# Sink keys inside the own-key tiles of batches 2 and 3, and a written TensorE order, in a sliding-window attention and FFN kernel

## The chip, the core and the metric

The kernel runs on one core of one Trainium2 chip. A core has five engines with one in-order instruction stream each: TensorE (PE: matmuls and their weight loads), VectorE (DVE), ScalarE (ACT), GpSimd (POOL) and SyncE (SP). POOL, SP and ACT also issue DMA transfers, which sixteen DMA engines carry out. The metric is the device time of one execution in microseconds (us), the median of several runs.

## The reference

There are four batches of eight heads, 768 queries each, with a head size of 64. A query sees the keys of its window (itself and the 127 before it) and the first four keys of the sequence, the sinks. The attention output of all heads, as 3072 tokens by 512, goes through a gated feed-forward net.

```python
scores = scale * np.matmul(q, k.transpose(0, 1, 3, 2))
is_sink = pos[None, :] < int(n_sink)              # n_sink = 4
in_window = (rel >= 0) & (rel < int(window))      # rel = query - key, window = 128
scores = np.where(is_sink | in_window, scores, -1000000000.0)
a = np.exp(scores - np.max(scores, axis=-1, keepdims=True))
a = a / (np.sum(a, axis=-1, keepdims=True) + 1e-09)
attn = np.matmul(a, v)                            # 4 x 8 x 768 x 64
# x = attn as (3072, 512)
h = (x @ w1) * (x @ w2) @ w3                      # w1, w2: 512 x 1024, w3: 1024 x 1024
out = h @ w_out                                   # w_out: 1024 x 512
```

## The kernel before

Everything is cast to bf16 and multiplied on TensorE. `w3 @ w_out` is folded into one 1024 x 512 matrix first: `fold_w3` (task `t3`, four transposes of 128 x 128 each) and `fold_mm` (task `fm`, two matmuls of 512 columns each). Then each batch goes through attention, the two gate products (task `g`, four matmuls for 128 hidden units and one chunk of tokens) and the projection (task `p`, eight matmuls of 512 columns for 128 tokens).

Attention works on scores with keys in the partitions. Queries and keys arrive as tokens by head dimensions and are turned by TensorE (`transposes`, task `tpk`, eight transposes for 128 tokens; batches 0 and 1) or by DMA (`transposes_dma`, tasks `tdk` and `tdq`, issued on SP; batches 2 and 3, list `XPOSE`). Two heads share the 128 rows of the array, 64 rows each, so score matmuls come in pairs that run side by side. For a tile `t` of 256 queries and a pair of heads `r`, `scores` (task `sc`, L254) multiplies the key blocks before, at and after the tile's middle: six matmuls for a `t` above 0, four for `t` = 0. ACT takes the exponential, DVE multiplies with a 0/1 mask, and `values` (task `av`, L334) multiplies the result with the values. A value row carries a 1 behind its 64 numbers, so column 65 of the product is the sum by which DVE divides (`rec`, L354 and L357). Batch 0 has a variant of the two in blocks of 128 queries (L273, L298).

The sinks go another way in tiles with `t` above 0. `sink_scores` (task `ss`, L237) multiplies the four sink keys of all eight heads, laid out in `ksbd`, in four matmuls of 32 columns of weights; ACT takes the exponential into `es`, and `values` adds one matmul of 130 columns per 128 queries, from `es` and the sink values `vs`. `sink_keys` and `sink_values` prepare `ksbd` and `vs` on DVE.

The attention output is turned again, by TensorE (task `xt`, batch 0) or by DMA (`x_transposes_dma`, task `xd`, L374, on SP), since the gate products take it with the dimensions in the partitions.

POOL casts while it loads: `load_qkv` (L108) issues one DMA each for 128 tokens of k, q and v. The weights to be folded come over SP as fp32 (`load_raw`) and are cast by DVE and ACT. Before the first of them has come, `keep_busy` (L464) multiplies the zeros of `idle`, which is `ksbd[3]`, set first of all by DVE (L173 and L174).

The order of all engines but POOL comes from a planner in the kernel (`plan`, L674). Each task has stages with an engine and an estimated duration, the tasks that it comes after, and the loads that it needs, with landing times from `landings` (L484). The planner walks through time; ACT, DVE and SP take what is ready first, and `pe_pick` (L689) chooses for TensorE the task with the least wait and the best priority, with a margin for `av` and a pace for `sc`. The planner's times set only the order; on the chip each engine goes through its list and waits by semaphores. Score tiles share two PSUM buffers (`ps_sc`), everything else four (`ps_mm`, ring `mm`).

Of the kernel before, what the change touches and what calls it, by code (L numbers as in the profile page):

```python
# [21 lines left out]
def kernel(  # L22
# [13 lines left out]
    nc = tc.nc  # L36
# [19 lines left out]
    SINKS = (1, 3)  # L56
# [15 lines left out]
    vc = const.tile([P, B, D], FP32, name="vc")  # L72
    maskt = const.tile([P, 2, 512], BF16, name="maskt")
# [5 lines left out]
    wo_sb = wp.tile([P, KFF, DM], BF16, name="wo_sb")  # L79
# [9 lines left out]
    vN = per_batch("vN", [P, NB, H, VS], 3)  # L89
# [5 lines left out]
    ksbd = per_batch("ksbd", [P, 648], 4)  # L95
    vs = per_batch("vs", [P, H, D + 1], 4)
    es = per_batch("es", [P, 512], 2)


    def rows(src, b, kb):  # L100
        return src[b, :, kb * P:(kb + 1) * P, :].rearrange("h p d -> p h d")
# [5 lines left out]

    def load_qkv(b, kb):  # L108
        for src, dst in zip(kqv, (heads(kN[b][:, kb, :]), heads(qN[b][:, kb, :]), vN[b][:, kb, :, 0:D])):
            nc.gpsimd.dma_start(out=dst, in_=rows(src, b, kb))  # L110
# [18 lines left out]
    def load(what, *i):  # L129
        if what == "qkv":  # L130
            if i[1] == 0:
                nc.gpsimd.memset(vN[i[0]][:, :, :, D:D + 1], 1.0)
            for kb in range(i[1], i[2]):
                load_qkv(i[0], kb)
        elif what == "w3":
            load_rows(w3_sb, what, *i)
        elif what == "wo":
            load_rows(wo_sb, what, *i)
        else:
            for dst, src in ((w1_sb, moe_w1), (w2_sb, moe_w2)):  # L140
                load_w(dst, src, i[0] * 256, i[1] * 256)
# [7 lines left out]
    order = [("w3", 6, 8), ("qkv", 0, 0, 1), ("qkv", 0, 1, 2), ("w3", 5, 6), ("qkv", 0, 2, 3),  # L149
             ("qkv", 0, 3, 4), ("w12", 0, 1), ("w12", 1, 2), ("w12", 2, 3), ("w12", 3, 4), ("qkv", 0, 4, 5),  # L150
             ("qkv", 0, 5, 6), ("qkv", 1, 0, 6), ("qkv", 2, 0, 6), ("qkv", 3, 0, 6)]

    nudge = {("g", 0, 1, 5, 0): -300, ("g", 1, 0, 6, 1): 60, ("p", 3, 5, 256): -300, ("g", 2, 0, 3, 0): -300}
# [19 lines left out]
    idle = ksbd[B - 1]  # L173
    nc.vector.memset(idle[:], 0.0)  # L174
# [3 lines left out]
    for b in range(B - 1):  # L178
        nc.vector.memset(ksbd[b][:], 0.0)
# [4 lines left out]
    m4 = maskt[:].rearrange("p v (a c q) -> p (v a) c q", c=2, q=P)  # L184
    nc.gpsimd.affine_select(m4[:, :, 0, :], m4[:, :, 0, :], compare_op=ALU.is_ge, fill=0.0,
                            base=-1, pattern=[[0, 4], [-1, P]], channel_multiplier=1)
    nc.gpsimd.affine_select(m4[:, :, 1, :], m4[:, :, 1, :], compare_op=ALU.is_ge, fill=0.0,
                            base=0, pattern=[[0, 4], [1, P]], channel_multiplier=-1)
    nc.gpsimd.memset(maskt[0:4, 0, P:3 * P], 1.0)
# [7 lines left out]
    for b in range(B):  # L197
        nc.gpsimd.tensor_copy(vs[b][:, :, D], ones_s[:])
    for h in range(H):
        r0 = 32 * (h // 2) + 4 * (h % 2)  # L200
        nc.sync.dma_start(out=vc[r0:r0 + 4, :, :], in_=v[:, h, 0:4, :].rearrange("b s d -> s b d"))
    if hold:
        nc.gpsimd.tensor_copy(spent[:], casts[hold - 1][1][:, 0:1])
    for x in order:
        if x[0] != "qkv" or x[1] == 0:
            load(*x)

# [10 lines left out]
    def transposes_dma(src, dst, kb):  # L218

        nc.sync.dma_start_transpose(out=dst[:, :, kb * P:(kb + 1) * P], in_=src[:, kb, :])  # L220
        yield
# [31 lines left out]

    def scores(b, r, t):  # L254
# [13 lines left out]
        mk = maskt[:, min(t, 1):min(t, 1) + 1, c0:].to_broadcast([P, 2, 512 - c0])  # L268
# [4 lines left out]
    def block_scores(b, j, r0, r1):  # L273
# [3 lines left out]
        for r in range(r0, r1):  # L277
            for s, kb in enumerate(kbs):
                for e in range(2):
# [8 lines left out]
        n, v, c = len(kbs) * P, min(j // 2, 1), (P, 2 * P)[j] if j < 2 else 0  # L288
        nc.vector.tensor_mul(am[:].rearrange("p e (r x) -> p (e r) x", x=n),
                             ex[:].rearrange("p e (r x) -> p (e r) x", x=n),  # L290
                             maskt[:, v:v + 1, c:c + n].to_broadcast([P, 2 * (r1 - r0), n]))
# [6 lines left out]
    def block_values(b, j, r0):  # L298
# [17 lines left out]
        rec = work.tile([P, 2, 2, 1], FP32, tag="rec", name="rec")  # L316
        nc.vector.reciprocal(rec[:], av[:, :, :, D:D + 1])
        if i == 0 and r0 == 0:
            xns[b, t] = work.tile([P, 2, NP, 2, D], BF16, tag="xn", bufs=3, name="xn")
        nc.vector.tensor_mul(xns[b, t][:, i, r0:r0 + 2, :, :], av[:, :, :, 0:D],  # L320
                             rec[:].to_broadcast([P, 2, 2, D]))
# [12 lines left out]
    def values(b, r, t):  # L334
# [18 lines left out]
        rec = work.tile([P, 2, 2, 1], FP32, tag="rec", name="rec")  # L353
        nc.vector.reciprocal(rec[:], av[:, :, :, D:D + 1])  # L354
        if r == 0:
            xns[b, t] = work.tile([P, 2, NP, 2, D], BF16, tag="xn", bufs=3, name="xn")
        nc.vector.tensor_mul(xns[b, t][:, :, r, :, :], av[:, :, :, 0:D],  # L357
                             rec[:].to_broadcast([P, 2, 2, D]))
# [15 lines left out]
    def x_transposes_dma(b, t, i):  # L374

        q0 = t * 256 + i * P
        nc.sync.dma_start_transpose(out=xT[b][:, :, q0:q0 + P],
                                    in_=xns[b, t][:, i].rearrange("p r e d -> p (r e d)"))
# [24 lines left out]
    def fold_w3(i, j0, j1):  # L403
# [5 lines left out]
        if i not in w3T:  # L409
            w3T[i] = (flat((kN, qN)[i - 4][1], "k s")[:, 2048:3072].rearrange("p (k n) -> p k n", n=P)  # L410
                      if i in (4, 5) else work.tile([P, KFF, P], BF16, tag="w3t", bufs=4, name="w3t"))
# [52 lines left out]
    def keep_busy(n):  # L464

        pz = ps_mm.tile([P, 512], FP32, tag="mm", name="pz")
        for _ in range(n):
            nc.tensor.matmul(pz[:], idle[:, 0:P], idle[:, 0:512], start=True, stop=True)
# [5 lines left out]
    def service(what, *i):  # L474
        if what == "qkv":
            return [(0.95 if i[0] == 0 else 0.87, 0.845 if 6 * i[0] + kb < 14 else 2.1, [(x, i[0], kb)])
                    for kb in range(i[1], i[2]) for x in "kqv"]
# [6 lines left out]
    def landings(RAW=2.0, POOL=3.0, DGE=1.3, RAMP=(0.75, 1.0)):  # L484
# [6 lines left out]
        while any(at[n] < len(q) for n, q in queues.items()):  # L491
# [11 lines left out]
            for n in busy:  # L503
# [3 lines left out]
                if left[n][at[n]] <= 0.0:  # L507
                    lag, keys = queues[n][at[n]][2:]
                    for key in keys:
                        arrive[key] = now + lag + min(2.5, max(0.0, 0.25 * (now - 36.0))) + min(3.0, max(0.0, 0.1 * (now - 70.0)))  # L510
# [51 lines left out]
    last_av = []  # L562
    for b in range(B):
        for t in range(NT):
# [3 lines left out]
            for kb in kbs:  # L568
# [5 lines left out]
                else:  # L574
                    qk.append(("tpk", b, kb))
                    task(qk[-1], 1, transposes(b, kb), [("pe", 0.45), ("dve", 0.65)],
                         war, [("k", b, kb), ("q", b, kb)], "mm")
            if t == 0:
# [35 lines left out]
            for r in range(NP):  # L614
                after = list(qk)
                if b >= 2 and t == 0:
# [214 lines left out]
```

## Time and profile before

| what | value |
|---|---|
| three runs | 195.87, 197.02 and 197.35 us, median 197.02 |
| span of the profiled execution (first to last instruction) | 193.9 us |
| DVE busy | 114.7 us, 59% of the span |
| ACT busy | 103.0 us, 53% |
| POOL busy | 75.2 us, 39% |
| queue of POOL's DMAs | 12.33 MB, 90.4% of 16 engines' span |
| queue of SP's DMAs | 16.49 MB, 40.5% |
| HBM | 29.39 MB read, 6.29 MB written |

The profiled execution has no time of its own beside its span; against the three runs, 2.0 to 3.5 us lie around the span. The profile's page gives busy time per engine, a row of tenths for 40 slices of the span, and the chain of work that ended last. The chain in order of time has a row for each stretch: start, length, engine, what was written, line, number of instructions. A matmul's duration in the trace overlaps with that of the next, so the cost of one in a stream is read from the length of a stretch over its count. A few matmul records are missing from the trace, so some counts are one too low.

### The profile page before, as it was taken

The page shows a single profiled execution, that of the slowest core. Times are in us where ns is not written, and L with a number is a line of the kernel's source. Part 1 is how long each engine was busy: PE and PEld are TensorE (multiplying, and loading weights), DVE is VectorE, ACT ScalarE, POOL GpSimd, SP SyncE. Part 2 cuts the span into 40 slices and gives each one's busy share as a digit, 9 for nine tenths or more (in the row PEclk, how much of TensorE's full clock was granted, in tenths as well). Part 3 has the DMA queues.
Part 4 walks back from the last instruction along what each step waited for, and adds up shares of the span by engine and source line. Part 5 has one row for each costly group of instructions (what it writes and reads, how often), then busy time and mean ns, then how long its engine had stood idle before and what let it go on. Part 6 is the DMA issues. An engine that isn't in the chain of part 4 may idle for free.

```text
span 193.9 us, 4599 instructions
## 1 busy us (share of the span) xinstructions
PE 186.7 (96%) x1808; PEld 123.1 (63%) x1825; DVE 114.7 (59%) x277; ACT 103.0 (53%) x175; POOL 75.2 (39%) x102
## 2 busy tenths in 40 slices
PE   7899999999999999999999999999999999999994
PEld 2344556898867787588799556654666565655542
DVE  5554687856699887678785435660588564444100
ACT  4052289743766876575764627352884563333232
POOL 5189987688899863443155351000000000000000
PEclk9999999999999999999999999999999999999999
DMA  6999999999999999999999999999320432000144
GB/s 219 372 391 179 170 159 196 196 161 153 155 147 194 195 150 119 154 133 238 144 140 158 144 164 209 190 153 205 113 52 6 110 110 55 0 0 3 68 162 149
DMA packets 108021, 29.17 MB, mean 150 GB/s; under 512 B 98656, under 2 KB 103904, under 8 KB 108000
## 3 DMA queue, kind: packets, MB, share of 16 engines
q0 software_dynamic: 79520, 12.33, 90.4%
q1 hardware_dynamic: 28336, 16.49, 40.5%
q8 instruction: 14, 0.23, 0.5%
q10 hardware_dynamic: 144, 0.07, 0.1%
q14 instruction: 7, 0.06, 0.1%
HBM read 29.39 MB, written 6.29 MB: 184 GB/s over the span
## 4 chain that ended last, share of the span: by engine, by line
PE 88%; DMA 8%; SPq 1%; issue 1%; DVE 0%; POOL 0%; ACT 0%
PE pg L390 44%; PE po L451 21%; PE av L350 7%; PE sc L260 5%; DMA ab<-in_moe_w_out_dram 4%; DMA w_sb<-in_moe_w_dram 4%; PE tp L213 3%; PE pw L437 3%; PE av L313 1%; PE sc L281 1%; PE tp L407 1%; PE ph L437 1%; SPq L165 1%; PE sp L242 1%; PE xt L329 1%
## 5 line engine op out<-in xcount | busy, mean ns | idle before, releaser
L390 PE MATMUL pg<-xT,w_sb 128*128 128x256 bf16 (+1 forms) x640 | 90.8, 294 | 0.0
L390 PEld LDWEIGHTS <-w_sb 128*128 128x128 bf16 x640 | 59.8, 98 | 20.7 <-issue 1.7
L397 ACT COPY a_sb<-pg 128x256 f32<-128x256 f32 (+1 forms) x80 | 33.3, 416 | 37.4 <-PE pg L390 24.1
L394 DVE TENSOR_TENSOR ab<-a_sb,pg 128x256 bf16<-128x256 f32 (+1 forms) x80 | 37.6, 471 | 23.8 <-PE pg L390 21.2
L451 PE MATMUL po<-w3o,ab 128*128 128x512 bf16 (+2 forms) x196 | 42.7, 362 | 0.5
L265 ACT ACTIVATE ex<-sc 128x1024 bf16<-128x1024 f32 (+1 forms) x40 | 37.9, 963 | 5.3 <-PE sc L260 4.6
L269 DVE TENSOR_TENSOR am<-ex,maskt 128x1024 bf16<-128x1024 bf16 (+1 forms) x40 | 25.3, 646 | 12.8 <-ACT ex L265 12.8
L451 PEld LDWEIGHTS <-ab 128*128 128x128 bf16 x208 | 19.1, 98 | 19.7 <-issue 0.2
L455 ACT COPY w_sb<-po 128x512 f32<-128x512 f32 (+2 forms) x25 | 14.1, 564 | 26.2 <-PE po L451 24.1
L110 POOL DMA_DIRECT2D kN<-in_k_dram x24 | 21.6, 900 | 13.1 <-DMA qN<-in_q_dram 9.2
L110 POOL DMA_DIRECT2D qN<-in_q_dram x24 | 21.8, 909 | 11.9 <-DMA vN<-in_v_dram 7.7
L110 POOL DMA_DIRECT2D vN<-in_v_dram x24 | 21.4, 893 | 8.6 <-DMA kN<-in_k_dram 7.6
L357 DVE TENSOR_TENSOR xn<-av,rec 128x256 bf16<-128x256 f32 x40 | 17.0, 425 | 1.4
L350 PE MATMUL av<-vN,am 128*128 128x65 bf16 x296 | 16.9, 193 | 0.0
L350 PEld LDWEIGHTS <-am 128*128 128x128 bf16 x296 | 14.5, 97 | 2.3 <-issue 0.2
L354 DVE RECIPROCAL rec<-av 128x4 f32<-128x4 f32 x40 | 7.2, 180 | 12.3 <-PE av L350 12.2
L260 PE MATMUL sc<-kqT 64*128 64x128 bf16 (+1 forms) x216 | 11.6, 238 | 0.1
L350 PE MATMUL av<-vs,es 128*128 128x130 bf16 x56 | 11.1, 221 | 0.0
L285 ACT ACTIVATE ex<-sc 128x1024 bf16<-128x1024 f32 x7 | 7.1, 1045 | 5.3 <-PE sc L281 5.3
L260 PEld LDWEIGHTS <-kqT 64*128 64x128 bf16 x216 | 6.9, 94 | 4.0 <-issue 3.4
L215 DVE COPY kqT<-tp 128x1024 bf16<-128x1024 bf16 x12 | 8.3, 689 | 1.8 <-PE tp L213 1.7
L437 PE MATMUL ph<-wo_sb,w3t 128*128 128x512 bf16 x32 | 8.1, 379 | 0.4 <-DVE w3t L412 0.3
(70 smaller groups left out, 126.5 us busy)
## 6 DMA issues: line engine op xcount, KB each, us to landing
out_dram<-w_sb SPq DMA_DIRECT2D x20, 256.0 KB
kN<-in_k_dram POOLq DMA_DIRECT2D x24, 128.0 KB, 8.6
qN<-in_q_dram POOLq DMA_DIRECT2D x24, 128.0 KB, 8.2
vN<-in_v_dram POOLq DMA_DIRECT2D x24, 128.0 KB, 8.6
w_sb<-in_moe_w_dram POOLq DMA_DIRECT2D x9, 256.0 KB, 8.5
ab<-in_moe_w_dram SPq DMA_DIRECT2D x4, 512.0 KB
ab<-in_moe_w_out_dram SPq DMA_DIRECT2D x2, 512.0 KB
out_dram<-w_sb SPq DMA_DIRECT2D x7, 128.0 KB
```

The source lines that it names most:

```text
L110: nc.gpsimd.dma_start(out=dst, in_=rows(src, b, kb))
L260: nc.tensor.matmul(sc[:, e, c:c + n], kT[b][hp, r, kb * P:(kb + 1) * P], qT[b][hp, r, qb * P:qb * P + n], start=True, stop=True)
L265: nc.scalar.activation(ex[:, :, c0:], sc[:, :, c0:], ACTF.Exp, scale=scale)
L269: nc.vector.tensor_mul(am[:, :, c0:], ex[:, :, c0:], mk)
L350: nc.tensor.matmul(o, lhs, rhs, start=(n == 0), stop=(n == len(todo) - 1), skip_group_check=True)
L357: nc.vector.tensor_mul(xns[b, t][:, :, r, :, :], av[:, :, :, 0:D], rec[:].to_broadcast([P, 2, 2, D]))
L390: nc.tensor.matmul(pg[:], w_sb[:, kk, dt * P:(dt + 1) * P], xT[b][:, kk, tk], start=(kk == 0), stop=(kk == NP - 1))
L394: nc.vector.tensor_mul(ab[b][:, dt, tk], gate_a.pop((b, c, dt))[:], pg[:])
L397: nc.scalar.copy(a_sb[:], pg[:])
L437: nc.tensor.matmul(po, w3T[i][:, j, :], wo_sb[:, j, :], start=(j == 0), stop=(j == KFF - 1))
L451: nc.tensor.matmul(po[:], ab[b][:, kk, m * P:(m + 1) * P], w3o[:, kk, n0:n1], start=(kk == 0), stop=(kk == KFF - 1))
L455: (nc.vector.tensor_copy if n0 == DM // 2 else nc.scalar.copy)(o_sb, po[:])
```

## The change

In batches 2 and 3 (`LATE`) the sinks have no path of their own any more. Queries go in seven blocks of 128, 128, 64 and four times 112 (`CUTS`), in three units of 3, 2 and 2 blocks. For each block from the third on, the keys are a tile `kown` of 128 that holds the 4 sink keys and the 124 keys up to the block's end, and the plain 128 keys before the block. The values match: `vN` is loaded in seven slots that end where the blocks end, so that two of them overlap with others; `own_values` saves plain slots to `vp` and overwrites rows 0 to 3 of the slots with the sink values. `late_scores` has eight matmuls in each unit (columns of 256, 128, 64 and 64 in the first, four times 112 in the others, each for two heads), `late_values` ten or eight of 65 columns. `sink_scores`, `sink_keys` and `sink_values` run for batches 0 and 1 only. The token chunks of the gate products become 320 and 448 instead of 384 and 384. Masks for the new tiles are made on POOL, six of the selects behind the first loads. The first unit needs the turned keys and queries of three blocks of 128, where the first tile before needed two; the second needs blocks 1 to 4.

TensorE's order is no longer picked but read from a list of 350 tasks, `TURNS`, and `LEAN` shifts the rank of 42 stages on the other engines. The zeros for `keep_busy` are now those of `ksbd[1]`, which DVE sets behind `ident`, `maskt` (now 1536 wide, 1024 before) and `vc`.

```diff
-    CHUNKS = [[(256 * i, 256 * i + 256) for i in range(3)]] * 2 + [[(0, 384), (384, 768)]] * (B - 2)
+    SINK = 4
+    LATE = range(2, B)
+    CUTS = (0, 128, 256, 320, 432, 544, 656, 768)
+    QB = list(zip(CUTS, CUTS[1:]))
+    UNITS = ((0, 1, 2), (3, 4), (5, 6))
+    SPANS = [(QB[u[0]][0], QB[u[-1]][1]) for u in UNITS]
+    KEYS = [(max(0, q1 - P), q1) for _, q1 in QB]
+
+    CHUNKS = [[(256 * i, 256 * i + 256) for i in range(3)]] * 2 + [[SPANS[0], (SPANS[1][0], S)]] * (B - 2)
...
+    VSLOTS = ((0,), (1,), (2, 3), (4,), (5,), (6,))
+
     def load_qkv(b, kb):
...
+        for s in VSLOTS[kb] if b in LATE else (kb,):
+            t0, t1 = KEYS[s] if b in LATE else (kb * P, (kb + 1) * P)
+            nc.gpsimd.dma_start(out=vN[b][:, s, :, 0:D], in_=rows(v, b, t0, t1))
...
-                nc.gpsimd.memset(vN[i[0]][:, :, :, D:D + 1], 1.0)
+                nc.gpsimd.memset(vN[i[0]][:, :, :, D:VS], 1.0)
...
-    idle = ksbd[B - 1]
-    nc.vector.memset(idle[:], 0.0)
+    idle = ksbd[1][:, 0:512]
     nc.vector.memset(ident[:], 1.0)
     nc.vector.memset(maskt[:], 1.0)
     nc.vector.memset(vc[:], 0.0)
-    for b in range(B - 1):
+    for b in (1, 0):
         nc.vector.memset(ksbd[b][:], 0.0)
...
+    def own_keys(b, u):
+
+        if u < 0:
+            nc.vector.tensor_copy(kown[b][:, :, :, 0:SINK],
+                                  kT[b][:, :, 0:SINK].rearrange("p r (o x) -> p r o x", o=1)
+                                  .to_broadcast([P, NP, 5, SINK]))
+        elif u == 0:
+            nc.vector.tensor_copy(kown[b][:, :, 0, SINK:], kT[b][:, :, KEYS[2][0] + SINK:KEYS[2][1]])
+        else:
+            for s in UNITS[u]:
+                nc.vector.tensor_copy(kown[b][:, :, s - 2, SINK:], kT[b][:, :, KEYS[s][0] + SINK:KEYS[s][1]])
+        yield
+
+    def own_values(b, u):
+
+        s0, s1 = ((2, 3), (3, 5), (5, 6))[u]
+        nc.vector.tensor_copy(vp[b][:, s0 - 2:s1 - 2], vN[b][:, s0:s1])
+        yield
+        s1 += u == 2
+        nc.vector.tensor_copy(vN[b][0:SINK, s0:s1], vN[b][0:SINK, 0:1].to_broadcast([SINK, s1 - s0, H, VS]))
         yield
...
+    def late_scores(b, r, u):
+
+        if u == 0:
+            todo = [(P, kT[b][:, r, 0:P], 0, 2 * P), (3 * P, kT[b][:, r, P:2 * P], P, P),
+                    (64, kT[b][:, r, P:2 * P], 2 * P, 64), (0, kown[b][:, r, 0, :], 2 * P, 64)]
+            n = 512
+        else:
+            todo, n = [], 448
+            for i, s in enumerate(UNITS[u]):
+                q0 = QB[s][0]
+                todo += [(224 * i, kT[b][:, r, q0 - P:q0], q0, 112), (224 * i + 112, kown[b][:, r, s - 2, :], q0, 112)]
+        sc = ps_sc.tile([P, 2, 512], FP32, tag="sc", name="sc")
+        for c, keys, q0, m in todo:
+            for e in range(2):
+                hp = slice(64 * e, 64 * e + 64)
+                nc.tensor.matmul(sc[:, e, c:c + m], keys[hp], qT[b][hp, r, q0:q0 + m], start=True, stop=True)
+        yield
...
+    def late_values(b, r, u):
...
+            if u == 0:
+                add(0, P, P, 0)
+                add(1, 2 * P, P, 0)
+                add(1, 3 * P, P, 1)
+                add(2, 0, P, 2)
+                add(2, 64, P, 1)
+            else:
+                for i, s in enumerate(UNITS[u]):
+                    add(i, 224 * i, 112, 2 - s)
+                    add(i, 224 * i + 112, 112, s)
...
+    TURNS = [("t3", 0, 1), ("t3", 0, 0), ("t3", 2, 0), ("fm", 2, 0), ("t3", 4, 0), ("fm", 0, 0), ("t3", 2, 1), ("fm", 2, 1),
...
+             1), ("g", 0, 1, 2, 0), ("g", 0, 1, 2, 1), ("g", 0, 1, 1, 1), ("tpk", 0, 5), ("g", 0, 1, 3, 0), ("g", 0, 1, 4,
...
+             0), ("g", 0, 1, 5, 0), ("tpk", 1, 0), ("g", 0, 1, 5, 1), ("av", 0, 0, 2), ("tpk", 1, 1), ("sc", 0, 2, 2), ("sc", 0,
...
+             0), ("g", 1, 0, 2, 1), ("g", 1, 0, 4, 0), ("sc", 2, 0, 0), ("sc", 2, 1, 0), ("g", 1, 0, 4, 1), ("g", 1, 0, 3,
...
+             3, 1, 7, 1), ("p", 3, 1), ("p", 3, 5, 256), ("p", 3, 3), ("p", 3, 2), ("p", 3, 4), ("p", 3, 5), ("p", 3,
+             5, 384)]
...
         def pe_pick():
-            best = None
-            for k in tasks.values():
...
+            if len(line) == len(TURNS):
+                return None
+            k = tasks[TURNS[len(line)]]
...
-                queue[e].append((at + HOP, YIELD.get(k["name"][0], 0.1), us, k))
+                queue[e].append((at + HOP, YIELD.get(k["name"][0], 0.1) + LEAN.get((k["name"], i + 1), 0.0), us, k))
```

More of the change, by code (lines that the diff above doesn't have):

```diff
@@ L94, with rows @@
     ab = per_batch("ab", [P, KFF, S], 2)
[L95 to L101, printed above, removed]
+    vp = [None] * 2 + [inp.tile([P, 4, H, VS], BF16, tag="wo", bufs=1, name=f"vp_{b}") for b in LATE]
+    kown = [None] * 2 + [inp.tile([P, NP, 5, P], BF16, tag=f"kown{b % 2}", bufs=1, name=f"kown_{b}") for b in LATE]
+    ksbd = [inp.tile([P, 648], BF16, name=f"ksbd_{b}") for b in range(2)]
+    vs = [inp.tile([P, H, D + 1], BF16, name=f"vs_{b}") for b in range(2)]
+    es = [inp.tile([P, 512], BF16, name=f"es_{b}") for b in range(2)]
+    def rows(src, b, t0, t1):
+        return src[b, :, t0:t1, :].rearrange("h p d -> p h d")
     def heads(ap):
@@ L467, in keep_busy @@
         for _ in range(n):
-            nc.tensor.matmul(pz[:], idle[:, 0:P], idle[:, 0:512], start=True, stop=True)
+            nc.tensor.matmul(pz[:], idle[:, 0:P], idle, start=True, stop=True)
     arrive = {}
@@ L577, with turned @@
                          war, [("k", b, kb), ("q", b, kb)], "mm")
+            if b in LATE:
+                def turned(what, kbs):
+                    if (b, 0) in XPOSE:
+                        return [("td" + x, b, kb) for kb in kbs for x in what]
+                    return [("tpk", b, kb) for kb in kbs]
+                if t == 0:
+                    task(("ko", b, -1), 0, own_keys(b, -1), [("dve", 0.2)], turned("k", (0,)) + war)
+                mine = ((2,), (2, 3, 4), (4, 5))[t]
+                late.append((b, t, turned("k", mine), turned("kq", ((0, 1, 2), (1, 2, 3, 4), (3, 4, 5))[t]), war))
+                continue
             if t == 0:
@@ L615 @@
                 after = list(qk)
-                if b >= 2 and t == 0:
-                    after += [("g", b - 2, len(CHUNKS[b - 2]) - 1, dt, 1) for dt in range(KFF)]
                 lead = r % 2 == 0
```

206 lines of the change are left out of this document (138 added, 68 removed), and 58 rows, old and new, of tables (LEAN, TURNS).

## The prediction

> **What bounds the kernel now.** I read the page first: the span, the busy time of each engine and the two rows of tenths.
>
> ```profile
> span 193.9 us, 4599 instructions
> PE 186.7 (96%) x1808; PEld 123.1 (63%) x1825; DVE 114.7 (59%) x277; ACT 103.0 (53%) x175; POOL 75.2 (39%) x102
> PE   7899999999999999999999999999999999999994
> DMA  6999999999999999999999999999320432000144
> ```
>
> TensorE is busy for 96%, idle only in the first slices; DVE and ACT have 40% to spare. DMA is full up to slice 28, about 140 us. So the time is TensorE's work plus what it waits for, and a load that comes late is the likeliest wait. TensorE's own waits:
>
> ```profile
> PE tp L407 <- DVE w_sb L417: 0.7, 2, 0.5
> PE tp L407 <- DMA w_sb<-in_moe_w_dram: 0.4, 1, 0.4
> PE sc L281 <- DVE kqT L215: 0.4, 1, 0.4
> ```
>
> The last of these is at about 22 us; behind it TensorE waits for nothing. Then the chain in order of time, whose stretches give the price of each kind of work, and the start of TensorE's timeline:
>
> ```profile
> 31.41 0.43 PE pw L437 x2
> 52.66 0.55 PE tp L213 x8
> 82.39 0.44 PE sc L260 x8
> 92.32 0.55 PE sc L260 x12
> 92.87 0.22 PE sp L242 x4
> 102.45 5.24 PE pg L390 x48
> 108.24 0.22 PE sp L242 x4
> 130.41 0.18 PE av L350 x6
> 130.59 5.18 PE po L451 x24
> 139.65 0.33 PE sp L242 x4
> 142.22 0.36 PE av L350 x10
> 150.05 0.76 PE pg L390 x4
> 159.36 19.50 PE pg L390 x120
> 188.65 2.36 PE po L451 x20
> ```
>
> ```profile
> 1.33 4.73 PE L468 MATMUL pz<-ksbd 128*128 128x512 bf16 x12 [1.33 <-DVE ksbd L174]
> 6.21 0.62 PE L407 MATMUL tp<-ident,w_sb 128*128 128x128 bf16 x8
> 18.21 0.40 PE L407 MATMUL tp<-ident,w_sb 128*128 128x128 bf16 x4 [0.40 <-DMA w_sb<-in_moe_w_dram]
> 19.96 0.39 PE L213 MATMUL tp<-ident,kN 128*128 128x128 bf16 x4
> ```
>
> **Prices.** A matmul of the gate products takes 5.24/48 = 0.109 for 256 columns and 19.50/120 = 0.1625 for 384, so (0.1625 - 0.109)/128 = 0.42 ns a column and about 2.5 ns each besides. One of 512 columns takes 5.18/24 = 0.216, one of 65 columns 0.18/6 = 0.030, one of 130 columns (0.36 - 8 x 0.030)/2 = 0.06. Score matmuls run in pairs: two units of 384 pair columns take 0.44 and two of 512 take 0.55, which is 0.43 ns a pair column and 0.11 on top. Coming back costs 0.11 too (four matmuls of 384 take 0.76 behind scores, 4 x 0.1625 = 0.65 elsewhere). So each change of shape costs 0.11. The eight transposes at 52.66, behind scores, are 0.45 without it. Task by task: `t3` 0.22, `fm` 0.43, `tpk` 0.45, `g` 0.437 (256) and 0.65 (384), `p` 1.73.
>
> **TensorE's work, old and new.** Sink scores of batches 2 and 3 go: 0.22 + 0.22 + 0.33 less three changes of shape, 0.43. Values: four of 0.18 and eight of 0.36 per batch become four of 0.30 (ten matmuls of 65 columns) and eight of 0.24 (eight), 3.60 against 3.12, so 0.9 less for two batches with the rounding. Scores: 768 + 1024 + 1024 columns per pair of heads become 1024 + 896 + 896, the same sum, in 96 matmuls for 64; at 0.43 ns a pair column that is nothing, about 0.1 with the small remainders. Gate chunks of 320 and 448 cost 4 x (0.136 + 0.189) = 1.30 a pair as 2 x 0.65 do now. I count 60 changes of shape in the new list; the trace has 58: +0.2. Sum: -0.43 - 0.9 + 0.1 + 0.2 = about -1.0.
>
> **Where that is kept.** Because the order is fixed, I read down the list with these prices and hold it against the loads. Before the first `tpk` the list has 19 `fm` and 12 `t3`; the trace has 17 and 12 done at 19.96. Two more `fm` put it at 20.8. From there to the `tpk` of batch 1's second block lie 29 `g` (12.7), 13 `fm` (5.6), 7 `tpk` (3.1), 9 `sc` (1.9), 9 `av` (2.5), 4 `t3` and 4 `xt` (1.8), 2 `ss` (0.2) and 19 changes (2.1): 29.9. So TensorE stands there at 50.7. Before, it came there at 52.66, having done more gate work first. That block's queries are loaded by POOL:
>
> ```profile
> 44.34 0.88 POOL L110 DMA_DIRECT2D qN<-in_q_dram  x1 [0.29 <-issue]
> qN<-in_q_dram POOLq DMA_DIRECT2D x1, 128.0 KB, 7.1
> ```
>
> The first row is the issue, the second the DMA issue with KB and time to landing: it lands at 44.34 + 7.1 = 51.4 to 51.5, and TensorE waits for it until then, with all that stands behind it in the list. What remains is 67 `g` of 256 (29.3), 32 of 320 (17.4), 32 of 448 (24.2), 24 `p` (41.5), 38 `sc` (7.6), 39 `av` (10.9), 5 `tpk`, 2 `xt` and one `ss` (2.9) and 41 changes (4.5): 138.2. Priced in the same way, the old list from 19.96 gives 169.8; it took 191.0 - 0.2 (the last matmul's drain) - 19.96 = 170.9, of which 0.4 is the wait above. The other 0.7 in 171 become 0.6 in 138. TensorE ends at 51.5 + 138.2 + 0.6 = 190.3 against 190.8. With unrounded terms the gain is 0.6. The tail is the same: the last piece is still 128 columns of `p` and its copy on ACT.
>
> **The start.** The dummies of `keep_busy` wait for a memset that now stands behind three others:
>
> ```profile
> 1.24 0.17 DVE L175 MEMSET ident<- 128x128 bf16 x1
> 1.57 0.91 DVE L176 MEMSET maskt<- 128x1024 bf16 x1 [0.16 <-issue]
> 2.48 0.27 DVE L177 MEMSET vc<- 128x256 f32 x1
> ```
>
> With 1536 instead of 1024 that one takes 1.4; with `ident` and half of `vc` (0.3) and the gap of 0.16 the dummies begin 1.8 later, at about 3.2, and, twelve in 4.73, end near 7.9, where the first fold began at 6.21. On the way to 18.2 TensorE has idle stretches (0.7 and 0.4 in the waits above) and five more dummies of 0.216 to give. Between 0 and 1.8 late I take 0.4. It costs nothing, since TensorE would wait 0.8 at batch 1's second block anyway; without that cover it costs 0.4, at most 1.8.
>
> **The other engines.**
>
> ```profile
> L412 DVE COPY w3t<-tp 128x512 bf16<-128x512 bf16 x12 | 4.7, 420 | 5.4 <-PE tp L407 5.4
> ```
>
> ```profile
> 1.48 0.29 POOL L181 TENSOR_SCALAR_AFFINE_SELECT ident<-ident 128x128 bf16<-128x128 bf16 x1 [0.98 <-DVE ident L175]
> 2.56 0.64 POOL L185 TENSOR_SCALAR_AFFINE_SELECT maskt<-maskt 128x512 bf16<-128x512 bf16 x1 [0.79 <-DVE maskt L176]
> ```
>
> DVE gets twelve copies per batch for `kown`, `vp` and the sink rows. The nearest row is the copy of 512 bf16 at 0.42, and none of them is over twice that: I take 6 per batch in some 45, covered by 40% idle; at twice the price the cover still holds. But DVE now stands in line for a DMA: `own_keys` waits for turned keys, and gate products queue behind it, with four PSUM buffers as TensorE's cover. ACT loses three exponentials of the sinks. POOL makes six more masks and larger memsets at about 39 us, some 2.4 by the two rows (64 to 224 wide). Loads land 7.1 after issue there, so the DMA queue has work meanwhile: 0, at worst 1 on the load at 44.34.
>
> **The wait that I do charge.** Batch 2's first unit needs three turned blocks where the tile before needed two. SP issues the turns of the queries of batch 2's third and fourth block, and of batch 3's third, fifth and sixth, here:
>
> ```profile
> 76.31 1.52 SPq L220 DMA_TRANSPOSE kqT<-qN  x1
> ...
> 84.03 1.24 SPq L220 DMA_TRANSPOSE kqT<-qN  x1
> ...
> 115.54 1.23 SPq L220 DMA_TRANSPOSE kqT<-qN  x1
> ...
> 127.48 1.64 SPq L220 DMA_TRANSPOSE kqT<-qN  x1
> ...
> 133.39 1.54 SPq L220 DMA_TRANSPOSE kqT<-qN  x1
> ```
>
> No row shows their landing. The scores at 92.32 used the one issued at 84.03 without a wait, so it took at most 8.3; SP's own 1.2 is the lower end. Batch 2's third block lands between 77.8 and 84.6. Read down with the same prices, the list has 32.7 between batch 1's second block and these scores: TensorE is there at 51.5 + 32.7 = 84.2. DMA is full in this stretch, so I take the upper end: 0.4 of wait, which everything behind it inherits. Sum: -0.6 + 0.4 = -0.2. The execution on the page has a span of 193.9, so 193.7; put against the median of 197.02, 196.8.
>
> One more load of v in batch 2 and one in batch 3 cost what a load takes there:
>
> ```profile
> 82.07 0.87 POOL L110 DMA_DIRECT2D kN<-in_k_dram  x1 [1.47 <-PE av L350]
> ...
> 116.70 0.87 POOL L110 DMA_DIRECT2D vN<-in_v_dram  x1 [0.39 <-DMA kN<-in_k_dram]
> ```
>
> These are the first and last of 18: 34.6/17 = 2.0 each. Batch 2's fourth block and all after it come 2 later, batch 3's fifth and sixth 4. With the same 8.3, batch 3's third, fifth and sixth block are there by 125.8, 139.8 and 145.7 at the latest; the list has 75.0, 88.3 and 96.8 between batch 1's second block and the scores that want them, so with both waits it is there at 126.9, 140.2 and 148.7. It costs nothing, and what each is later than these is paid in full. One more `xd` per batch takes SP 1.2 like the rows above, in a queue that waits for work by then: nothing.
>
> **The rivals.** First, small pairs are no cheaper than large ones: the trace has no pair under 128 columns (128 x 0.43 = 55 ns). If pairs of 64 and 112 take the same, sixteen pairs of 64 lose 0.027 and sixty-four of 112 lose 0.007 each: +0.9, 197.7. For it speaks that each brings its own weights; against it, that a full-height matmul of 65 columns with its own weights takes 30 ns. The Trainium skill, "TensorE: Matmul & The Clock Gate", section "Back-to-back issue gap", goes further: in a stream of weight loads and matmuls the spacing of one is about 81 ns at 128 columns, because the load has to be paid. By that figure the eight matmuls of a late unit would take 0.65 instead of 0.2, an estimate of 10.8 more over 24 units. This trace does not agree: its stretches give 30 ns at 65 columns.
>
> Second, slower: the turned blocks of batch 2 come late. Place: its first scores in the list. Price: a microsecond for each by which the third block lands behind 84.2. It decides when a transpose there takes 10 instead of at most 8.3, or SP issues it 2 later: then +2.4 in place of +0.4, 198.8. For it: DMA is at 9 tenths there, the list leaves no way round, and the second unit follows with one load more. Against it: POOL and SP issue the same work up to that block.
>
> Third, faster: the loads are not the floor. If batch 1's second block lands a microsecond earlier and batch 2's third by 83, both waits go, TensorE keeps its 1.0 and the start gains the 0.4 for which it waited at 18.21: 197.02 - 1.4 = 195.6. Against it: POOL and DMA do nothing less before that load.
>
> Fourth, the list brings nothing and costs nothing because other engines set the pace: the waits charged above grow to the gain, 197.0. It is inside the forecast's own range.
>
> **How the numbers follow.** The forecast has 0.55 with the fourth in it, its own range 196.2 to 197.5; small pairs 0.12; late blocks 0.17; early loads 0.16. The range leaves out the far half of the fast and of the slow case: 195.4 to 198.9. A measurement of this kernel can tell about 1% (its three runs lie 0.75% apart). Faster by over 1% means under 195.0, the far part of the early loads: 0.09. Slower by over 1% means over 199.0, half of the late blocks and some for a place that I don't see: 0.14. Within: 0.77.
>
> **What would show it.** Right: the `tp` of batch 1's second block starts near 51.5 and waits for DMA; the new list's last `po` ends near 190.6; score stretches of the last units cost 0.19 a unit; the fold begins near 7.9. Wrong: a wait of over 1 us before batch 2's or 3's scores, a stretch of late scores over 0.25 a unit, many short waits of `av` for the mask (DVE in line behind a transpose), or a first `tpk` past 21.6, from where the late start costs its full length.

## The result, and the profile after

| | before | changed |
|---|---|---|
| median of 8 runs each, side by side | 196.70 us | 198.15 us |
| lowest to highest | 195.87 to 197.47 | 197.66 to 199.70 |
| ratio to before, 95% interval | | 1.0103 [1.0067, 1.014] |
| span of the profiled execution | 193.9 us | 196.3 us |
| end of the last `po` stretch | 191.01 us | 193.08 us |

Medians, ranges and ratios here and below are of runs in the chip's faster state; a few runs in its slower state (a lower granted clock, or a time over 1.5% above the kernel's fastest run) are left out.

The changed kernel is 1.0% slower, 1.45 us, where 0.2 less was forecast. Line numbers below are those of the changed kernel: `scores` for the late batches is L327, `late_values` L362, the transposes of `tpk` L249, the gate products L510, the projection L571, `keep_busy` L588. In kernels with one or two lines added they move by as much.

First the page of the changed kernel, span, busy time and tenths, and then all of TensorE's waits:

```profile
span 196.3 us, 4745 instructions
PE 189.5 (97%) x1880; PEld 126.5 (64%) x1880; DVE 121.3 (62%) x293; ACT 102.6 (52%) x172; POOL 79.5 (41%) x111
PE   3999999999999999999999999999999999999993
DMA  6999999999999999999999999999720202420034
```

```profile
PE pz L588 <- DVE ksbd L194: 3.2, 1, 3.2
PE tp L527 <- DVE w_sb L537: 0.2, 1, 0.2
```

TensorE does 55 more matmuls by its weight loads (1880 against 1825; 17 matmul records of the kernel before are missing), is busy 2.8 us longer than before (189.5 against 186.7), and behind 12 us its list has no wait of 0.2 or more: no load, no turned block, no mask. So the lost time isn't a wait behind the start; it lies in the start itself and in the length of the work. The chain in order of time (start, length, engine, what was written, line, number of instructions) says where:

```profile
3.22 5.18 PE pz L588 x12
8.40 0.45 PE tp L527 x8
...
22.01 0.45 PE tp L249 x8
...
52.12 0.45 PE tp L249 x8
...
84.77 0.55 PE sc L327 x16
...
88.05 0.30 PE av L362 x10
...
106.22 0.50 PE sc L327 x16
...
148.24 0.39 PE av L362 x8
...
162.94 0.81 PE av L362 x16
...
184.39 8.69 PE po L571 x56
193.10 0.27 ACT w_sb L575
```

Read against the prediction: the first `tpk` stands at 22.0 (21.85 in TensorE's timeline, the view that has 19.96 for the kernel before) instead of 20.8 to 21.2, and the `tp` of batch 1's second block at 52.12 instead of 51.5. The late scores cost what was forecast (0.50 for two units with one change of shape of 0.11, so 0.195 a unit), and so do ten matmuls of 65 columns (0.30); the weights of these ten have 128 columns throughout, since a block of 64 queries reads on into its neighbour (`add(2, 0, P, 2)`). But eight with 112-column weights take 0.39 instead of 0.24. TensorE's timeline in one such task (start, length; the lengths overlap, so the starts count) shows it matmul by matmul:

```profile
148.16 0.22 PE L362 MATMUL av<-vp,am 128*112 128x65 bf16 x1
148.21 0.22 PE L362 MATMUL av<-vN,am 128*112 128x65 bf16 x1
148.26 0.22 PE L362 MATMUL av<-vp,am 128*112 128x65 bf16 x1
```

One starts every 0.05 us; the prediction had 0.030. The groups by line and form (busy time and mean ns) name the difference in the weight loads of that line, 131 ns for 112 columns and 98 for 128:

```profile
L362 PEld LDWEIGHTS <-am 128*112 128x112 bf16 x128 | 8.4, 131 | 1.4
L362 PEld LDWEIGHTS <-am 128*128 128x128 bf16 x80 | 3.4, 98 | 0.8
```

So I had two suspects: the 112-column weights (128 matmuls at some 0.02 each, 2.6) and the dummies that begin at 3.22 (some 0.6). Two rivals speak of other things: that the smaller tiles cost something that wider weights wouldn't mend (64- and 112-column score pairs, more instructions), and that the written order is itself the loss.

### The profile page after: what moved, and what is told of

It is laid out like the page before. It is cut to its first block, busy times and chain, and to the rows that moved or that the text cites. A ratio compares the mean times of both kernels' runs of the same rounds, so it can differ in the third digit from the quotient of the medians.

```text
span 196.3 us, 4745 instructions
## 1 busy us (share of the span) xinstructions
PE 189.5 (97%) x1880; PEld 126.5 (64%) x1880; DVE 121.3 (62%) x293; ACT 102.6 (52%) x172; POOL 79.5 (41%) x111
## 4 chain that ended last, share of the span: by engine, by line
PE 96%; DVE 2%; issue 0%; ACT 0%
PE pg L510 43%; PE po L571 21%; PE av L362 5%; PE pw L557 4%; PE pz L588 3%; PE ph L557 3%; PE sc L327 3%; PE tp L249 3%; PE av L470 3%; PE sc L378 2%; PE tp L527 2%; PE av L433 1%; PE sc L400 1%; DVE maskt L191 1%; PE xt L449 1%; DVE kown L532 0%
## 5 line engine op out<-in xcount | busy, mean ns | idle before, releaser
L510 PE MATMUL pg<-xT,w_sb 128*128 128x256 bf16 (+2 forms) x640 | 91.9, 294 | 0.0
L510 PEld LDWEIGHTS <-w_sb 128*128 128x128 bf16 x640 | 60.0, 98 | 22.0 <-issue 0.8
L514 DVE TENSOR_TENSOR ab<-a_sb,pg 128x256 bf16<-128x256 f32 (+2 forms) x80 | 37.4, 473 | 34.8 <-PE pg L510 29.9
L517 ACT COPY a_sb<-pg 128x256 f32<-128x256 f32 (+2 forms) x80 | 32.8, 416 | 35.1 <-PE pg L510 29.9
L571 PE MATMUL po<-w3o,ab 128*128 128x512 bf16 (+2 forms) x208 | 44.4, 363 | 0.0
L571 PEld LDWEIGHTS <-ab 128*128 128x128 bf16 x208 | 19.3, 98 | 18.7 <-issue 0.2
L330 ACT ACTIVATE ex<-sc 128x896 bf16<-128x896 f32 (+1 forms) x24 | 22.0, 954 | 4.2 <-PE sc L327 4.2
L383 ACT ACTIVATE ex<-sc 128x1024 bf16<-128x1024 f32 (+1 forms) x16 | 15.1, 970 | 3.2 <-PE sc L378 3.0
L334 DVE TENSOR_TENSOR am<-ex,maskt 128x896 bf16<-128x896 bf16 (+1 forms) x24 | 15.0, 642 | 2.1 <-ACT ex L330 2.1
L362 PEld LDWEIGHTS <-am 128*112 128x112 bf16 (+1 forms) x208 | 11.8, 118 | 2.2
L362 PE MATMUL av<-vN,am 128*128 128x65 bf16 (+1 forms) x144 | 11.8, 204 | 0.0
L369 DVE TENSOR_TENSOR xn<-av,rec 112x256 bf16<-112x256 f32 (+1 forms) x24 | 11.3, 469 | 0.8
L588 PE MATMUL pz<-ksbd 128*128 128x512 bf16 x20 | 7.2, 525 | 3.2 <-DVE ksbd L194 3.2
L388 DVE TENSOR_TENSOR am<-ex,maskt 128x1024 bf16<-128x1024 bf16 (+1 forms) x16 | 10.0, 649 | 0.2 <-ACT ex L383 0.2
(85 smaller groups left out, 190.7 us busy)
```

Source lines behind the costliest of these rows:

```text
L330: nc.scalar.activation(ex[:, :, 0:n], sc[:, :, 0:n], ACTF.Exp, scale=scale)
L334: nc.vector.tensor_mul(am[:, :, 0:n], ex[:, :, 0:n], maskt[:, mv:mv + 1, 0:n].to_broadcast([P, 2, n]))
L362: nc.tensor.matmul(o, lhs, rhs, start=(x == 0), stop=(x == len(todo) - 1), skip_group_check=True)
L383: nc.scalar.activation(ex[:, :, c0:], sc[:, :, c0:], ACTF.Exp, scale=scale)
L510: nc.tensor.matmul(pg[:], w_sb[:, kk, dt * P:(dt + 1) * P], xT[b][:, kk, tk], start=(kk == 0), stop=(kk == NP - 1))
L514: nc.vector.tensor_mul(ab[b][:, dt, tk], gate_a.pop((b, c, dt))[:], pg[:])
```

## The experiments

Each experiment was timed together with the kernel before on one chip, and its ratio is to those runs. The experiments come from three chips, so between them the ratios are compared rather than the times.

**1. The value matmuls with 128-column weights.** In blocks of 112 the weights are read 16 columns further, into the neighbouring block or, at the end, into columns set to zero; the 16 further rows of the product are used by nothing. Everything else is the changed kernel.

```diff
+        if u:
+            nc.vector.memset(am[:, :, 448:464], 0.0)
...
-                todo.append((av[0:m, i, e, :], am[:, e, c:c + m], src))
+                todo.append((av[:, i, e, :], am[:, e, c:c + P], src))
```

> The changed kernel, but the value matmuls of the 112-query blocks load 128 columns of weights instead of 112 (the 16 further rows of the product are not used), with one small memset per unit on DVE for the last 16 columns. Theory A: a weight load of 112 columns is slower than one of 128, which is why a stretch of eight such matmuls takes 0.39 to 0.41 where 0.24 was expected. Then each of the 128 matmuls goes from 0.051 to 0.030, stretches of eight to 0.24, and 128 x 0.0215 = 2.7 goes from TensorE's stream: span 193.6, time about 195.4. Rival B: the stretches are long because the values wait for their masks or their PSUM buffer, and the loss is the late start: stretches stay at 0.39, time stays at 198.1, a little more for the memsets.

Measured: 195.85 us (194.48 to 196.57), ratio to before 0.9992 [0.9962, 1.0022], span 194.0. The chain has the same tasks as above:

```profile
147.24 0.24 PE av L364 x8
...
160.98 0.49 PE av L364 x16
...
182.11 8.69 PE po L573 x56
```

The eight take 0.24, the price that the prediction had used, and TensorE ends at 190.8 instead of 193.1. By the two ratios the weights carry 1.1% of the time, more than the whole loss. The median came 0.4 above the number expected, and the profile has a stall of 0.2 behind 138 us that the changed kernel did not have: TensorE stands there behind DVE, and DVE behind a load of v (experiment 6).

**2. The zeros for the dummies first.** The zeros of `ksbd[1]` are set first on DVE again, as in the kernel before.

```diff
     idle = ksbd[1][:, 0:512]
+    nc.vector.memset(ksbd[1][:], 0.0)
     nc.vector.memset(ident[:], 1.0)
...
-    for b in (1, 0):
-        nc.vector.memset(ksbd[b][:], 0.0)
+    nc.vector.memset(ksbd[0][:], 0.0)
```

> The changed kernel, but the memset of ksbd[1], whose zeros the dummies multiply, stands first on DVE again. Dummies begin at 1.3 instead of 3.2, the first fold at 6.2 instead of 8.2. Theory A (the start costs only what the loads don't hide): the first transposes of batch 0 go from 21.85 to between 20.3 and 21.0, but those of batch 1's second block can't start before its load lands at 51.4 and go from 52.1 to 51.5: gain 0.6, time 197.5, with a wait for DMA in TensorE's waits. Rival B (the late start is the whole loss): gain 1.8, time 196.3. Rival C (the fold waits for the casts and not for TensorE): gain 0.

Measured: 197.60 us (197.15 to 198.17), ratio 1.008 [1.0054, 1.0106], span 196.5. Its chain at the first `tpk` and at batch 1's second block, and its timeline at the one place where it then waits:

```profile
21.09 0.45 PE tp L249 x8
...
51.41 0.45 PE tp L249 x8
```

```profile
139.20 0.45 DVE L278 COPY vN<-vN 4x1152 bf16<-4x1152 bf16 x1 [1.82 <-DMA vN<-in_v_dram]
```

TensorE is 0.9 earlier at the first `tpk` and 0.7 earlier at the block. Of that, 0.2% of the time shows in the ratio to before (1.008 against 1.0103), some 0.5 us, and the two intervals overlap; in this profiled execution TensorE gave 0.6 back at 139 us, where it stood behind DVE and DVE behind a load of v. The wait for DMA at 51.4 that the prediction (and my expectation) put there doesn't appear. Of the 1.9 by which the dummies start earlier a part is lost again at once: with the zeros first, TensorE waits 0.7 at 18.29 for a load of weights to be folded.

**3. Both edits.**

> Both edits of the two runs beside it: weights of 128 columns for the values, zeros first. Theory A: the parts add up, 198.1 - 2.7 - 0.6 = 194.8, which is below the kernel before (196.7). Rival: TensorE's gain is taken back by waits for batch 2's and 3's turned keys, since it comes there 2 to 3 earlier: time between 195.5 and 197, with waits of score matmuls in TensorE's list of waits.

Measured: 196.09 us (194.38 to 197.29), ratio 0.9976 [0.9937, 1.0015], span 192.6. The profiled execution is as short as expected, and behind 9 us TensorE waits for nothing in it; the median isn't as short, and the runs lie 2.9 apart. The first scores of batch 2 stand at 83.62 here, without a wait for a turned block, so the rival's cause isn't there in this profile.

**4. What a matmul costs by the width of its weights.** Behind the last projection, eight streams of 48 matmuls on zeros, alone on TensorE, each with a weight load of its own: 128, 120, 112, 96, 64 and 32 columns of weights with 65 moving columns, then 128 and 112 with 128 moving columns. The output is complete before them; the time of the kernel is longer by them. It is a single execution, with a granted clock of 1.00.

```diff
+    def stream(mm):
+        pz = ps_mm.tile([P, 512], FP32, tag="mm", name="pz")
+        for _ in range(48):
+            mm(pz)
+
+    z = ksbd[1]
+    stream(lambda o: nc.tensor.matmul(o[0:128, 0:65], z[:, 0:128], z[:, 0:65], start=True, stop=True))
+    stream(lambda o: nc.tensor.matmul(o[0:120, 0:65], z[:, 0:120], z[:, 0:65], start=True, stop=True))
...
```

> The changed kernel with eight streams of 48 matmuls each behind its last projection, all on zeros, each matmul with its own weight load: 65 moving columns with weights of 128, 120, 112, 96, 64 and 32 columns, then 128 moving columns with weights of 128 and 112. Theory A (only a full load of 128 columns is fast, any narrower one takes a cycle a column): start to start 0.030 at 128, 0.055 at 120, 0.051 at 112, 0.044 at 96, 0.030 at 64 (where the moving columns set the pace) and 0.030 at 32; with 128 moving columns both 0.056, the load hidden. Rival B (a multiple of 32 or 64 is fast as well): 0.030 at 96 too. Rival C (112 isn't slow by itself): 0.030 at all widths.

The chain has one row for each stream, in that order:

```profile
193.49 1.46 PE pz L1020 x48
194.95 2.64 PE pz L1021 x48
197.59 2.48 PE pz L1022 x48
200.07 2.16 PE pz L1023 x48
202.23 1.64 PE pz L1024 x48
203.86 1.56 PE pz L1025 x48
205.42 2.79 PE pz L1026 x48
208.21 2.68 PE pz L1027 x48
```

Over 48 these are 0.030 us at 128 columns of weights, 0.055 at 120, 0.052 at 112, 0.045 at 96, 0.034 at 64 and 0.033 at 32. The full 128 are the cheapest; below, the spacing falls with the width, down to about 0.033 at 64 and 32, where 0.030 was expected. Rivals B and C are out: 96 columns aren't cheap, and 112 cost 0.052 with nothing else going on. With 128 moving columns the narrow load costs nothing more (0.056 against 0.058). The step from 128 to 112 columns alone gives 128 x (0.052 - 0.030) = 2.8 us for the late values.

**5. The new tiles in the old choice of order.** `pe_pick` of the kernel before in place of the list, without the shifted ranks.

```diff
-            k = tasks[TURNS[len(line)]]
...
+            for k in tasks.values():
...
+                wait = est - free["pe"]
+                key = (0.0 if wait < 0.05 else wait, k["prio"])
+                if best is None or key < best[0]:
+                    best = (key, k, est)
+            return best
...
-                queue[e].append((at + HOP, YIELD.get(k["name"][0], 0.1) + LEAN.get((k["name"], i + 1), 0.0), us, k))
+                queue[e].append((at + HOP, YIELD.get(k["name"][0], 0.1), us, k))
```

> The changed kernel with the tiles, loads and chunks of the change, but TensorE's order picked by the planner as in the kernel before (its priorities and paces, the old choice of the next task), without the written list and without the shifted ranks. Theory A (the list moves work but TensorE is busy in either order): within 0.7 of the changed kernel, 198.1 against 197.4 to 198.9. Rival B (the written list is what costs): 196.3 or less. Rival C (the list is worth something, since the old choice leaves waits with the new tiles): 199.5 or more, with waits in TensorE's list.

Measured: 201.63 us (200.33 to 202.16), ratio 1.024 [1.0194, 1.0287], span 199.7. Its longest wait on TensorE, the wait on DVE that stands behind it, and two stretches of its table of windows (busy time of PE, PEld, DVE, ACT and POOL, then the granted clock):

```profile
PE pg L510 <- DVE xn L477: 2.6, 1, 2.6
```

```profile
DVE vp L275 <- DMA vN<-in_v_dram: 3.7, 1, 3.7
```

```profile
75.00:78.00 3.00, 1.02 (x16) 0.55 (x12) 0.34 (x2) 1.32 (x2) 1.02 (x2) 1.00 1.36 103
78.00:81.00 3.00, 2.42 (x18) 1.93 (x20) 2.47 (x9) 1.20 (x2) 1.50 (x2) 0.54 1.75 151
```

DVE took the copy of batch 2's values first, stood in it until the load of v came, and `xn` of batch 1 and TensorE stood behind it. So the list isn't the loss: with these tiles the list and the shifted ranks together are worth 1.4% against the old choice (1.024 against 1.0103), 2.7 us. The place shown is the largest wait that they avoid; the runs don't divide the 2.7 further, nor between the list and the ranks.

**6. The last value copies later.** `own_values` of batch 3's third unit comes behind one more `av`, so that gate products aren't queued on DVE behind a load of v. Nothing else changes.

```diff
-             [("av", b - 1, NP - 1, NT - 1)] if b >= 3 else [],
+             ([("av", b - 1, NP - 1, NT - 1)] if b >= 3 else []) + ([("av", 3, 0, 1)] if (b, u) == (3, 2) else []),
```

> The changed kernel with one thing moved: DVE overwrites the sink rows of batch 3's last value slots (the two copies of the last own_values) some 14 us later, behind the first values of the unit before. In two of three profiles of kernels near this one DVE waited 1.5 to 1.8 at that copy for batch 3's last load of v, and TensorE then 0.4 to 0.7 behind it. Theory A (that wait differs from run to run and makes the spread of 197.7 to 199.7): median goes to about the lowest run, 197.5, spread under 1. Rival B (the spread has another cause): median 198.1, spread 2.

Measured: 197.84 us (196.86 to 199.38), ratio 1.0075 [1.0043, 1.0106], span 196.0. Rival B: at most 0.3 in the median, inside the intervals, and the runs lie as far apart as before (2.5, against 2.0). The two profiles that the expectation speaks of, of experiments 1 and 2, have TensorE waiting 0.2 and 0.6 behind that copy, and the changed kernel's own profile has no wait there.

**7. All three edits.**

> Weights of 128 columns, zeros first and the late copies together. Theory A: the parts add up; the run with the first two had 194.4 in its best run and 196.15 as a median, and without the wait of DVE for the last load the median comes near its best: 194.6, ratio to the kernel before 0.99, spread under 1.5. Rival B: the spread stays, 196.1, because with TensorE earlier another load or turned block comes late; its waits would name it.

Measured: 195.03 us (194.53 to 195.94), ratio 0.9935 [0.9906, 0.9964], span 193.3: 0.65% faster than the kernel before, with an interval below 1, and faster than the changed kernel. The three ratios taken alone are 1.1, 0.2 and 0.3% below the changed kernel's, together 1.6; this one is 1.7 below.

**8. Which of the three are needed.** Three kernels beside each other: without the zeros first, without the late copies, and all three once more.

> The kernel with 128-column weights and the two late value copies, but with the zeros again set behind ident, maskt and vc. Theory A: the late start is paid in full on the path, about 0.6 us at the first tpk (21.9 against 21.1), so the median lies 0.4 to 0.9 above that of the kernel with all three edits run beside it. Rival B: TensorE waits for loads further on and takes the start back, median within 0.2 of the kernel with all three edits. The PE waits show no wait behind 25 us in A.

> 128-column weights and zeros first, without the late value copies, timed on the same chip as the kernel with all three edits. Theory A: DVE's wait for the last load of v in batch 3, which stands ahead of gate products, costs about 1 us in the runs where that load is late; median 0.5 to 1.2 above the kernel with all three edits and a spread over 2.5. Rival B: the copies' place costs nothing that a median shows, and the 1.1 between the two earlier measurements was the chips; median within 0.4 of the kernel with all three edits.

> All three edits, the comparison for the two kernels beside it. Both theories: 194.6 to 195.4, ratio to the kernel before 0.990 to 0.996, spread under 2.

| | median | ratio to before |
|---|---|---|
| 128-column weights, late copies | 195.61 | 0.9962 [0.9925, 0.9999] |
| 128-column weights, zeros first | 195.45 | 0.9967 [0.9934, 1.0] |
| all three | 194.75 | 0.993 [0.9897, 0.9962] |

By the medians the zeros first are worth 0.9 and the late copies 0.7, as both theories A had it (by the ratios 0.3 and 0.4%, some 0.6 and 0.7 us). The intervals overlap, so that neither is shown by itself. Two of the expectations' details fell. Without the zeros first TensorE does wait behind 25 us, for 0.2 and 0.5:

```profile
27.72 0.40 PE L249 MATMUL tp<-ident,qN 128*128 128x128 bf16 x4 [0.15 <-DMA qN<-in_q_dram]
...
66.64 0.34 PE L472 MATMUL av<-vN,am 128*128 128x65 bf16 x6 [0.50 <-DVE kqT L251]
```

And without the late copies the runs lie 2.0 apart and not over 2.5. The timeline of that kernel (first DVE's row, then TensorE's) shows what the copies cost:

```profile
137.74 0.45 DVE L278 COPY vN<-vN 4x1152 bf16<-4x1152 bf16 x1 [2.08 <-DMA vN<-in_v_dram]
```

```profile
138.76 1.67 PE L512 MATMUL pg<-xT,w_sb 128*128 128x448 bf16 x8 [0.82 <-DVE ab L516]
```

DVE waits 2.1 for the load, and TensorE 0.8 for DVE. With all three edits the same happens one unit earlier, for 0.6:

```profile
125.33 0.46 DVE L275 COPY vp<-vN 128x1152 bf16<-128x1152 bf16 x1 [1.31 <-DMA vN<-in_v_dram]
```

```profile
126.24 0.70 PE L512 MATMUL pg<-xT,w_sb 128*128 128x320 bf16 x4 [0.64 <-DVE ab L516]
```

## Why the prediction was wrong

**The values, the step that failed.** The prediction priced a late unit at "eight of 0.24 (eight)" by 0.18/6 = 0.030 a matmul of 65 columns. Every row behind that price had weights of 128 columns, and 112 was taken for the same. It takes 0.39 (0.05 a matmul in the kernel, 0.052 alone), and 0.24 once the weights are 128 wide. The difference is 0.15 in the row of eight and 0.32 in the row of sixteen, so 16 x 0.16 = 2.6 us for the sixteen late tasks of that kind, where "0.9 less" stood for all values. With it the step's sign turns: 1.7 more. The one narrow-weight row in the trace of before, the sink scores with 32 columns, moves 256 or 512 columns, so it says nothing of a load beside only 65 moving columns. I did weigh whether small weights cost more, for the score pairs (the first rival, "small pairs are no cheaper"), where it wasn't so, and answered it with a row of full weights; for the values the question was not asked.

The Trainium skill has this rule in "TensorE: Matmul & The Clock Gate", section "Weight-path perf modes — Fast Weight Load (FWL) and DoubleRow": the fast load is on when the number of weights is 128 and the type isn't fp32. The runs agree: 98 ns against 131 a load, and a step from 0.030 to 0.055 between 128 and 120 columns. The prediction took another section of that page and found its 81 ns at 128 columns not borne out; the streams alone give 58.

**The start.** "It costs nothing, since TensorE would wait 0.8 at batch 1's second block anyway." The dummies begin at 3.22 and end at 8.40 (forecast about 3.2 and 7.9), and the first `tpk` at 22.0 is past the 21.6 from which the text let the late start cost its full length. So the size charged, 0.4, was too small, and the cover wasn't there either. The cover had been worked out with the landing of the kernel before, 7.1 after the issue. POOL's row of that load in the changed kernel, and its DMA issue:

```profile
44.55 0.91 POOL L122 DMA_DIRECT2D qN<-in_q_dram  x1
qN<-in_q_dram POOLq DMA_DIRECT2D x1, 128.0 KB, 5.8
```

It lands at 50.35, and TensorE comes at 52.12: nothing to wait for. A load's landing under traffic is not a constant of the place (5.8 here, 7.1 before), and one row of it was used as a floor. Against the 50.7 that was read down the list TensorE comes 1.4 late: about 0.7 by the start (experiment 2), and about 0.7 by the reading itself, since with the zeros first it comes at 51.41. The other profiles agree on the start: the block's `tp` stands at 51.63 to 52.49 in the five with late zeros (the changed kernel and experiments 1, 4, 6 and 8) and at 50.92 to 51.41 in the five with the zeros first.

**The waits charged further on.** The 0.4 for batch 2's third turned block did not come, since TensorE is at its first scores at 84.77, 0.6 later than forecast, and no wait is there; at 83.62 in experiment 3 there is none either. The 0.6 added for waits that the old trace had over its length did not come either.

**The sum.** From batch 1's second block to the end of the last `po`, less the drain of 0.2, the prediction had 138.2 + 0.6 + 0.4 = 139.2; the trace has 193.08 - 0.2 - 52.12 = 140.8. The 1.6 between them are the 2.6 of the weights, less the 0.4 and the 0.6, two charges that did not come and so hid a part of the error. With 0.6 before that block TensorE ends 2.2 late, at 192.9 against 190.7. With 128-column weights the same stretch is 190.80 - 0.2 - 52.03 = 138.6, with 0.2 of waiting in it: the rest of the reading down the list was right to half a per cent. Another 0.3 lies behind the last `po`, where the prediction had "the tail is the same": from there to the end of the span it is 3.2 in the changed kernel and 2.9 before. Why stays open.

The median of 198.15 lies inside the range of 195.4 to 198.9, and that is luck: its upper part stood for late turned blocks and dear small pairs, and neither came.

**What was right.** Scores of 0.195 a unit and no penalty for pairs of 64 or 112 columns: the first rival is false. The second, late turned blocks, is false in all of these kernels. The third, "the loads are not the floor", came true as to one of its causes, batch 1's second block landing a microsecond earlier, but TensorE was later still. The other engines kept up in the changed kernel itself. "DVE now stands in line for a DMA" was named with the turned keys as the cause; where it bit, with the old order and once TensorE was faster, it was the copies of the values, which the prediction counted only as 6 us of DVE's time.

**The measure.** The profiled executions differ by 2.4, the medians by 1.45. The profiled execution of the changed kernel took 198.03 with its span of 196.3, and in all eight runs 1.7 to 1.9 lie around the span. So before's span of 193.9 belongs to a run of about 195.6, 1.1 below its median: a typical run of the kernel before loses about 1 us that its one profile doesn't show. The 70 runs of it beside the experiments say the same more mildly: their spans have a median of 194.55, and 15 of them are 193.9 or less. The prediction set the sum against the median and so carried that microsecond along. What it is, and why the runs of several of these kernels lie 2.0 to 2.9 apart, stays open; the v loads in front of DVE's copies are a part of it at most (experiments 6 and 8).

## What to carry to other kernels

Ask of every price whether its rows have the same shape in both operands: a matmul with few moving columns can be paced by its weight load, and here a load of 96 to 120 columns cost more than one of all 128; so cut blocks to 128, or let the weights read on to 128 columns where nothing reads the further rows. Before a delay is called covered, set two times against each other, when the engine arrives and when the load lands, and let the landing vary by what the same load shows elsewhere. When an engine that others depend on gets a copy which waits for a DMA, list what is queued behind it; making TensorE faster turns that queue into the next wait.

## What the runs showed of the hardware

The jump lies at the last columns: 120 columns of weights cost more than 32 (0.055 against 0.033 us a matmul of 65 columns), and more than 128 (0.030).

A stall in mid-kernel can be paid twice. In experiment 5 TensorE was idle for about 2.6 us and then had a granted clock of 0.54 over the next 3 us, with eight gate products of 256 columns in 1.7 us, where 0.9 is usual. The Trainium skill, "TensorE: Matmul & The Clock Gate", section "Part 1: The HAM clock gate (the "warmup" mystery)", gives half the clock after an idle window of about 3.4 us; here 2.6 of idle was enough. Of the six runs of that kernel four have a mean granted clock of 0.990 or 0.991 and take 201.58 to 202.16 us, and two have 0.998 or 0.999 and take 200.33 and 200.96, so the second payment, about 1 us, seems not to come in every run. The stalls of 0.6 and 0.8 shown in experiment 8 did not lower the clock: it is 1.00 in the windows around them.
